# Turning the last token tiles and the shared expert blocks on TensorE, and taking weight conversions off the first batch's chain

## The chip, the cores and the metric

The kernel runs on one core of a Trainium2 chip. The metric is the device time of one execution in microseconds. PE below is the matrix engine (TensorE), PEld its weight load, DVE the vector engine, ACT the scalar engine, POOL the GpSimd engine, and SP the queue from which most transfers are issued, one after the other.

## What is computed

Three layers in a row: an attention with packed keys and values, a mixing layer with two Fourier transforms and a dense network, and a mixture of eight experts in which a token may take its predecessor's expert. All in float32.

```python
def attn(q, k, v, p):                      # 8 batches, 8 heads, 576 tokens, 64 wide; p: 32 packed rows
    packed = sm_attn(p, k, v)              # softmax attention
    return sm_attn(q, packed, packed)

def mix(x, w_ch1, w_ch2):                  # x: 8 x 576 x 512, w_ch1: 512 x 2048, w_ch2: 2048 x 512
    u = x + np.real(fft(fft(x, axis=1), axis=2))
    un = (u - mean(u)) / sqrt(var(u) + 1e-6)
    return u + maximum(un @ w_ch1, 0) @ w_ch2

def moe(x, w_gate, w_local, w1, w2):       # 8 experts, w1: 512 x 1024, w2: 1024 x 512
    for b, s in all tokens in order:
        fresh = argmax(x[b, s] @ w_gate)
        e = fresh if s == 0 or sigmoid(x[b, s] @ w_local) < 0.5 else prev_e
        prev_e = e
        out[b, s] = softmax(x[b, s] @ w_gate)[e] * (maximum(x[b, s] @ w1[e], 0) @ w2[e])
```

## The kernel before

Numbers are kept as pairs of float16 (high and low halves), so that a product takes three matmuls: high by high, high by low, low by high (PASS). The 4,608 tokens form 36 tiles of 128, called by their column 0 to 35; a batch has four whole tiles, and the rests of four batches together make two more (columns 16, 17 and 34, 35).

**First batch.** first_batch() is written in the order in which each engine runs it (the builder's scheduler is off there). It computes attention and mixing of batch 0. Its end is: P and Q products on PE (pq, L951), copies of Q to qs on ACT, combine(t) on DVE for tile pair t (L991: uu and ul are sums and differences of P and qs), stats(t) (mean and variance), level(t, j) (normalise to un, turn un with TensorE into the bank unt), high(t, j) and low(t, j) (the two float16 halves of the turned tokens, into `ut`). t is 0, 1 for 256 tokens each. While this runs, `weights(n)` draws n steps from the generator ch_weights (L281), which loads the mixing weights, chunk f of 16, unpacks them (k0, k1, k2 on DVE, L309 to L313), and lets split() (L277) make the halves of `w12`: high on ACT (L278), low on DVE (L279).

**Mixes.** Mix.mm1(f) makes a hidden chunk, 12 matmuls of 512 columns into hp (L1129); mm2(f) multiplies it back into acc (L1149). mm2 runs two chunks behind mm1. Between matmuls, tick() advances background generators by their rates: ch_weights at CW_RATE chunks' steps, attention of the next batch (attention(b + 1)), conversion of the expert weights into the DRAM tiles WS1 and WS2, after_mix of the mix before. From here on a scheduler places instructions, in the program's order unless an instruction has priority.

**Routing.** after_mix(tiles) (L1157) takes each finished tile: DVE finds its scale, ACT and DVE write its halves to a row tile `hl` (xh, three buffers, shared with the gathered rows xg), SP turns it with a DMA into `xt` (L1188, one buffer) and writes it to DRAM as XS (L1189). The logits of a tile are made from xt on PE (L1166, L1168), one tile behind. routing(gr) chooses experts and sorts tokens into blocks of 128, first for columns 0 to 17 and then, in finish_routing (after_mix of the last batch, columns 30 to 33, and routing(1)), beside the first expert blocks.

**Expert blocks.** The list `line` holds the 37 blocks in order: 34 with one expert and three shared by two experts of 64 tokens each (FIRST to FIRST + 2, which are 39 to 41). load_x gathers a block's rows and turns them by DMA (three blocks ahead); e1 (L1525) has 96 matmuls of 128 columns from `w1b` into ehp, e2 (L1586) 24 of 512 from `w2b` into eo. The loop over `line` issues e1 of block i + 1 before e2 of block i. Weight loads (L1517, four parts each) are issued by SP at places given by `first` and `second`. A shared block's e1_two (L1549) leaves its hidden rows hh unturned; turned(b) (L1570) turns them with 4 matmuls for each of four quarters (psum tile ht, copy to hx on ACT or DVE), and it runs inside e2 of the block before, between its matmuls.

Of the kernel before, what the change touches and what calls it, by code (L numbers as in the profile page):

```python
# [188 lines left out]
CW_RATE = 5  # L189
# [3 lines left out]
def _build(tc, nc, ctx, A, stop):  # L193
# [80 lines left out]
    held = []  # L274


    def split(dst_hi, dst_lo, src, scale):  # L277
        nc.scalar.activation(dst_hi, src, AF.Copy, scale=scale)  # L278
        nc.vector.scalar_tensor_tensor(dst_lo, src, scale, dst_hi, ALU.mult, ALU.subtract)  # L279

    def ch_weights():  # L281
# [15 lines left out]
        for f in range(16):  # L297
# [19 lines left out]
            split(w12[:, f, :, 0], w12[:, f, :, 1], t.rearrange("p (a n) -> p a n", a=2), 128.0)  # L317
# [408 lines left out]
    def first_batch():  # L726
# [201 lines left out]
        weights(5)  # L928
# [10 lines left out]
        weights(1)  # L939
# [36 lines left out]
        pq(1)  # L976
        x_mm(1, 1, psA)
# [13 lines left out]
        def combine(t):  # L991
# [3 lines left out]
            nc.vector.tensor_tensor(ul[R, :256], P[t][R, :256], qs[t][R, :256], op=ALU.subtract)  # L995
            if t == 0:
# [14 lines left out]
        def stats(t):  # L1011
# [10 lines left out]
            nc.gpsimd.tensor_tensor(out=rstd, in0=rstd, in1=mhalf, op=ALU.pow)  # L1022
            nbs[t] = wp.tile([128, 2], F32, tag="nb", name=f"nb0_{t}", bufs=2)
# [34 lines left out]
        weights(3)  # L1058
        combine(0)
        stats(0)  # L1060
        combine(1)
# [6 lines left out]
        stats(1)  # L1068
        level(1, 0)
        level(1, 1)  # L1070
        weights(1)
# [4 lines left out]
        combine(2)  # L1076
# [11 lines left out]
        split(wgh[:, :, 0], wgh[:, :, 1], wgf, 64.0)  # L1088
# [25 lines left out]
    class Mix:  # L1114
# [5 lines left out]
        def mm1(self, f):  # L1120
# [4 lines left out]
            hp = psM.tile([128, 512], F32, tag="h", name=f"hp{self.tiles[0][1]}_{f}")  # L1125
            n = 0
            for c in range(4):
                for (x, y) in PASS:
                    nc.tensor.matmul(hp[:, :ntok], w12[:, f, 0, x, 128 * c:128 * c + 128], ut[:, 4 * y + c, :ntok],  # L1129
                                     start=n == 0, stop=n == 11)  # L1130
                    n += 1
# [28 lines left out]
    def after_mix(tiles):  # L1160
# [12 lines left out]
        for j, (ut, col) in enumerate(tiles):  # L1173
# [311 lines left out]
    xg, xt, regs, hb = {}, {}, {}, {}  # L1485

# [38 lines left out]
    def e1(b, todo=()):  # L1525
# [3 lines left out]
        for fg in range(2):  # L1529
            hp = (psM, psO)[fg].tile([128, 512], F32, tag="ho"[fg], name=f"ehp{b}_{fg}")  # L1530
            for f in range(4):
                n = 0
                cols = slice(128 * f, 128 * f + 128)
                for c in range(4):
                    for (x, y) in PASS:
                        nc.tensor.matmul(hp[:, cols], w1b[r][:, 2 * c + fg, x, cols], xt[b][:, 4 * y + c],  # L1536
                                         start=n == 0, stop=n == 11, skip_group_check=True)
# [11 lines left out]
    def e1_two(b, todo=()):  # L1549
# [209 lines left out]
```

## Time and profile before

| | |
|---|---|
| median of 3 runs | 1425.25 us (1423.19 to 1433.6) |
| the profiled execution's own time | 1422.04 us |
| its span in the trace | 1420.0 us |
| mean granted PE clock, share of full speed | 0.987 |
| busy: PE, PEld, DVE, ACT, POOL | 1370.0, 791.2, 696.6, 516.1, 379.2 us |
| first batch's chain | 0 to about 62 us |
| end of the mixes, start of the expert blocks | about 983 us |

The first four numbers say how long it takes; the span leaves out about 2 us around the work. Busy times are sums of instructions' durations, so a busy engine may still run slowly: the granted clock says how fast PE was allowed to run in a stretch (1.0 is 2.4 GHz, 0.5 is 1.2 GHz). Views of the trace give for every instruction its start and duration and, in brackets, how long its engine had been idle before it and what released it.

### The profile page before, as it was taken

What the parts mean: (1) busy time and instruction counts of PE and PEld (TensorE: products, weight loads), DVE (VectorE), ACT (ScalarE), POOL (GpSimd) and SP (SyncE); (2) the same over time, 40 slices, a digit from 0 to 9 for tenths busy, and PEclk for the clock granted to TensorE, in tenths of its full rate; (3) what the DMA queues carried; (4) which work ended last, traced back from release to release, by engine and by line L of the source; (5) the groups of instructions that cost most, each with busy time, mean ns of one, the idle gap of its engine ahead of it and who ended that gap; (6) DMA issues with size and microseconds to landing.
All of it is one profiled execution on the core that took longest, in us unless ns stands there. A gap on an engine that the chain in (4) does not pass through costs nothing. (4 is left out here: it accounts for less than half of the span.)

```text
span 1420.0 us, 27686 instructions
## 1 busy us (share of the span) xinstructions
PE 1370.0 (96%) x10812; PEld 791.2 (56%) x10812; DVE 696.6 (49%) x1415; ACT 516.1 (36%) x950; POOL 379.2 (27%) x386
## 2 busy tenths in 40 slices
PE   7799999999999999999999999999999999999998
PEld 5553445444564544444544456446577777776654
DVE  5799856657534655665665755433561111111111
ACT  2443365554355545445445444211211111111111
POOL 1002243443422434343344252000121211212101
PEclk8999999999999999999999999999999999999999
DMA  7465384784567558558557457244969668858881
GB/s 262 160 211 197 91 237 124 172 237 121 137 171 209 156 150 214 142 147 219 139 153 197 121 148 166 58 194 129 261 145 318 180 190 250 264 149 239 280 275 44
DMA packets 223864, 257.67 MB, mean 181 GB/s; under 512 B 155887, under 2 KB 167279, under 8 KB 221040
## 3 DMA queue, kind: packets, MB, share of 16 engines
q1 hardware_dynamic: 217648, 236.44, 58.9%
q0 software_dynamic: 6080, 19.40, 4.2%
q8 instruction: 87, 1.43, 0.4%
q14 instruction: 49, 0.40, 0.1%
HBM read 267.52 MB, written 52.95 MB: 226 GB/s over the span
## 5 line engine op out<-in xcount | busy, mean ns | idle before, releaser
L1149 PE MATMUL acc<-w,ht 128*128 128x512 f16 x1728 | 409.5, 379 | 0.0
L1129 PE MATMUL hp<-ut,w 128*128 128x512 f16 x1536 | 365.9, 380 | 3.8 <-DMA ut<-unh 2.5
L1129 PEld LDWEIGHTS <-w 128*128 128x128 f16 x1920 | 183.1, 98 | 183.0 <-issue 11.4
L1149 PEld LDWEIGHTS <-ht 128*128 128x128 f16 x1728 | 165.7, 98 | 188.6 <-issue 8.6
L337 POOL TENSOR_TENSOR halfs<-stage,halfs 128x512 f16<-128x512 f32 x128 | 151.2, 1187 | 294.6 <-ACT halfs L336 279.0
L1597 PE MATMUL eo<-w2b,hx 128*128 128x512 f16 (+1 forms) x984 | 210.7, 382 | 0.0
L1536 PE MATMUL ehp<-xgt,w1b 128*128 128x128 f16 x3360 | 202.0, 220 | 3.2 <-DMA w1b<-WS 3.2
L1536 PEld LDWEIGHTS <-w1b 128*128 128x128 f16 x3360 | 194.0, 99 | 16.5 <-DMA w1b<-WS 3.7
L1545 DVE SCALAR_TENSOR_TENSOR hx<-ehp,hx 128x512 f16<-128x512 f32 x70 | 48.3, 691 | 294.5 <-ACT hx L1544 294.5
L1137 DVE SCALAR_TENSOR_TENSOR ht<-hp,ht 128x512 f16<-128x512 f32 (+1 forms) x160 | 101.2, 633 | 154.9 <-ACT ht L1136 153.9
L1136 ACT ACTIVATE ht<-hp 128x512 f16<-128x512 f32 (+1 forms) x160 | 88.1, 550 | 233.5 <-PE hp L1129 228.6
L1597 PEld LDWEIGHTS <-hx 128*128 128x128 f16 (+1 forms) x984 | 87.5, 100 | 99.9 <-issue 8.6
L1608 POOL DMA_INDIRECT out<-ys,sidx x38 | 41.0, 1079 | 291.3 <-ACT ys L1607 266.4
L1544 ACT ACTIVATE hx<-ehp 128x512 f16<-128x512 f32 x70 | 41.8, 597 | 163.7 <-PE ehp L1536 163.5
L1607 ACT ACTIVATE ys<-eo,scl 128x512 f32<-128x512 f32 x38 | 26.1, 687 | 170.5 <-PE eo L1597 170.5
L336 ACT CAST halfs<-stage 128x512 f16<-128x512 f32 x128 | 77.6, 615 | 9.3 <-DMA WS<-halfs 5.5
L1491 POOL DMA_INDIRECT xg<-XS,gidx x38 | 40.5, 1066 | 141.1 <-DVE sidx L1458 51.5
L335 ACT ACTIVATE stage<-stage 128x512 f32<-128x512 f32 x128 | 77.7, 623 | 0.2
L362 POOL TENSOR_TENSOR qh<-q,qh 128x1420 f16<-128x1420 f32 x12 | 34.6, 2882 | 51.6 <-ACT qh L361 51.5
L1129 PE MATMUL hp<-utr,w 128*128 128x256 f16 x384 | 47.1, 272 | 0.0
L574 PE MATMUL bp<-cst,eh 128*128 128x289 f16 (+1 forms) x168 | 26.2, 291 | 12.9 <-DVE lsum L1170 9.6
L539 POOL TENSOR_TENSOR eo<-ee 128x256 f32<-128x256 f32 (+1 forms) x21 | 17.0, 811 | 77.2 <-DVE ee L523 74.0
(408 smaller groups left out, 1388.2 us busy)
## 6 DMA issues: line engine op xcount, KB each, us to landing
w1b<-WS SPq DMA_DIRECT2D x156, 512.0 KB
w2b<-WS SPq DMA_DIRECT2D x156, 512.0 KB
stage<-in_w SPq DMA_DIRECT2D x64, 512.0 KB
WS<-halfs SPq DMA_DIRECT2D x128, 256.0 KB
q<-in_qd SPq DMA_DIRECT2D x16, 710.0 KB
v<-in_vd SPq DMA_DIRECT2D x16, 640.0 KB
k<-in_kd SPq DMA_DIRECT2D x16, 576.0 KB
XS<-xh SPq DMA_DIRECT2D x36, 256.0 KB
```

What stands on the lines that cost most here:

```text
L335: nc.scalar.activation(st[:, a], st[:, a], AF.Copy, scale=64.0 if k < 4 else 256.0)
L336: nc.scalar.copy(so[:, 0], st[:, a])
L337: nc.gpsimd.tensor_tensor(so[:, 1], st[:, a], so[:, 0], op=ALU.subtract)
L1129: nc.tensor.matmul(hp[:, :ntok], w12[:, f, 0, x, 128 * c:128 * c + 128], ut[:, 4 * y + c, :ntok], start=n == 0, stop=n == 11)
L1136: pace[1] = nc.scalar.activation(ht[:, 0, :ntok], hp[:, :ntok], AF.Relu).ins
L1137: pace[0] = nc.vector.scalar_tensor_tensor(ht[:, 1, :ntok], hp[:, :ntok], 0.0, ht[:, 0, :ntok], ALU.max, ALU.subtract).ins
L1149: nc.tensor.matmul(self.acc[j], ht[:, x, 128 * j:128 * j + 128], w12[:, f, 1, y], start=f == 0 and n == 0, stop=f == 15 and n == 2)
L1536: nc.tensor.matmul(hp[:, cols], w1b[r][:, 2 * c + fg, x, cols], xt[b][:, 4 * y + c], start=n == 0, stop=n == 11, skip_group_check=True)
L1544: nc.scalar.activation(ht[:, fg, 0], hp, AF.Relu)
L1545: nc.vector.scalar_tensor_tensor(ht[:, fg, 1], hp, 0.0, ht[:, fg, 0], ALU.max, ALU.subtract)
L1597: nc.tensor.matmul(op[rows], h[:, f // 4, x, c0 + rows.start:c0 + rows.stop], w2b[r + a][:, f, y], start=n == 0, stop=n == 23, skip_group_ ...
L1608: nc.gpsimd.indirect_dma_start(out=A["out"], out_offset=bass.IndirectOffsetOnAxis(ap=sidx[:, b:b + 1], axis=0), in_=ys, in_offset=None, bo ...
```

## The change

There are three edits. **A:** in first_batch, fewer weight steps stand ahead of the chain: six are drawn before the halves copies, none between Q and combine(0), and split() yields between its high and its low half, so the two can be placed apart. combine and stats become generators whose parts interleave; level(t, 0) runs on DVE for both t. begin(0) and begin(1) start mix chunks f = 0 and 1 on the first 256 tokens, before tile pair 1 is turned; mm1 then does the other 256 columns of these two. The rate CW_RATE goes from 5 to 6, since a chunk now has one step more. **B:** the last batch's four tiles (columns 30 to 33) are turned by four matmuls for each half and a copy on ACT and one on DVE, instead of a DMA; the last tile's logits follow after one step instead of four. **C:** the turns of a shared block go beside e1 of the next block, one quarter after each odd f, each placed behind the newest matmul of that e1, instead of beside e2 of the block before.

```diff
-CW_RATE = 5
+CW_RATE = 6
     def split(dst_hi, dst_lo, src, scale):
         nc.scalar.activation(dst_hi, src, AF.Copy, scale=scale)
+        yield
         nc.vector.scalar_tensor_tensor(dst_lo, src, scale, dst_hi, ALU.mult, ALU.subtract)
...
-        weights(5)
+        weights(6)
         halves(0, 0)
...
-        weights(1)
         qs, P, Q = {}, {}, {}
...
         pq(1)
+        weights(1)
         x_mm(1, 1, psA)
...
-            if (t, j) == (1, 0):
+            if j == 0:
                 nc.vector.tensor_scalar(un, ...
...
+        def begin(f):
+            hp = begun[f] = psM.tile([128, 512], F32, tag="h", name=f"hp0_{f}")
+            n = 0
+            for c in range(4):
+                for (x, y) in PASS:
+                    nc.tensor.matmul(hp[:, :256], w12[:, f, 0, x, 128 * c:128 * c + 128], ut[:, 4 * y + c, :256],
+                                     start=n == 0, stop=n == 11, skip_group_check=True)
+                    n += 1
-        weights(3)
-        combine(0)
-        stats(0)
-        combine(1)
+        whole(combine(0))
+        norm0, norm1, second = stats(0), stats(1), combine(1)
+        next(norm0)
+        next(second)
+        whole(norm0)
         level(0, 0)
...
         low(0, 1)
-        stats(1)
+        whole(second)
+        next(norm1)
+        weights(1)
+        whole(norm1)
+        begin(0)
         level(1, 0)
         level(1, 1)
-        weights(1)
+        weights(3)
+        begin(1)
         high(1, 0)
...
     # Mix.mm1
+            hp = begun.pop(f, None)
+            c0 = 0 if hp is None else 256
...
-                    nc.tensor.matmul(hp[:, :ntok], w12[...], ut[:, 4 * y + c, :ntok], ...
+                    nc.tensor.matmul(hp[:, c0:ntok], w12[...], ut[:, 4 * y + c, c0:ntok], ...
...
+    def turn_half(dst, src, nm, x):
+        tp = att(nm)
+        for c in range(4):
+            cols = slice(128 * c, 128 * c + 128)
+            nc.tensor.matmul(tp[:, cols], src[:, cols], idh, start=c == 0, stop=True, skip_group_check=True)
+        if x:
+            nc.vector.tensor_copy(dst, tp)
+        else:
+            nc.scalar.copy(dst, tp)
...
-            nc.sync.dma_start_transpose(out=xt, in_=hl)
+            if by_pe:
+                for x in range(2):
+                    turn_half(xt[:, 4 * x:4 * x + 4], hl[:, 512 * x:512 * x + 512], f"xtp{col}_{x}", x)
+            else:
+                nc.sync.dma_start_transpose(out=xt, in_=hl)
...
-        for _ in range(4):
+        for _ in range(1 if by_pe else 4):
             yield
         logits(tiles[-1][1])
...
     # e1, after the 12 matmuls of one f
+                if f % 2:
+                    next(beside, None)
...
     # turned
+                with tc.issue_after(newest[0]) if newest[0] is not None else nullcontext():
+                    turn_half(ht[:, fg, x], hh[:, fg, x], f"ht{b}_{fg}_{x}", x)
...
     # e2
-            if beside is not None and 2 <= f:
-                next(beside, None)
...
-    last = after_mix(prev.tiles)
+    last = after_mix(prev.tiles, True)
...
     # open_one(i), the e1 of line[i]
+        beside = turned(line[i - 1]) if i and line[i - 1] >= FIRST else iter(())
+        (e1_two if b >= FIRST else e1)(b, todo("e1", i), beside)
+        for _ in beside:
+            pass
```

What this does to the engines' orders is shown at three places. A row is a line of the program, the operation, and output<-inputs with the shape; numbers behind a name tell its batch, tile or chunk, and its allocation. Lines of the changed program stand one to some forty higher.

**The chain's head in the first batch.** First DVE before the change, around the first instruction of combine(0) (L994); raw1, halfs, stage and w12 belong to the weight conversion:

```order
L313 SCALAR_TENSOR_TENSOR raw1_177<-raw1_177,halfs_132 128x1024
L279 SCALAR_TENSOR_TENSOR w12_130<-raw1_177,w12_130 128x2x512
L309 TENSOR_SCALAR halfs_132<-stage_131 128x1024
L311 SCALAR_TENSOR_TENSOR halfs_132<-stage_131,halfs_132 128x1024
L994 TENSOR_TENSOR uu0_0_435<-P0_0_383,qs0_0_384 128x256
```

Then DVE of the change, where combine(0) is L996 to L1006 and X0_0 is added in stats(0):

```order
L315 SCALAR_TENSOR_TENSOR raw1_177<-raw1_177,halfs_132 128x1024
L996 TENSOR_TENSOR uu0_0_434<-P0_0_381,qs0_0_382 128x256
L997 TENSOR_TENSOR ul0_0_433<-P0_0_381,qs0_0_382 128x256
L1000 SCALAR_TENSOR_TENSOR ul0_0_433<-qs0_0_382,sgn_85,P0_0_381 128x256
L1006 SCALAR_TENSOR_TENSOR uu0_0_434<-qs0_0_382,sgn_85,P0_0_381 128x256
L1019 TENSOR_TENSOR uu0_0_434<-uu0_0_434,X0_0_1_366 128x512
```

And ACT in front of the same place, before the change (L932 copies halves, L969 to L973 make qs of tile pair 0):

```order
L932 ACTIVATE big0_256<-bp0_1_1_321 128x288
L278 ACTIVATE w12_130<-raw1_177 128x2x512
L969 COPY qs0_0_384<-zd0_382 1x257
L972 COPY qs0_0_384<-P0_0_383 128x255
L973 COPY qs0_0_384<-zd0_382 1x257
```

and with it, down to the copy for tile pair 1 (L964):

```order
L934 ACTIVATE big0_256<-bp0_1_1_321 128x288
L970 COPY qs0_0_382<-zd0_380 1x257
L973 COPY qs0_0_382<-P0_0_381 128x255
L974 COPY qs0_0_382<-zd0_380 1x257
L902 ACTIVATE big0_256<-att0_2_399 128x4x32
L964 COPY qs0_1_385<-P0_1_384 128x255
L279 ACTIVATE w12_130<-raw1_177 128x2x512
```

The low half of chunk 1 and the unpacking of chunk 2 (three DVE instructions) no longer stand between DVE's L313 and combine(0), and the high half of chunk 1 has moved behind the qs copies of both tile pairs on ACT.

**SP while the last tiles are routed.** SP before, from the last part of w1b for the third block on; xt31 to xt33 are the last batch's turned tiles, xh their row tiles, xgt a block's turned rows:

```order
L1517 DMA w1b2_10097<-WS1_128 128x2048
L1188 DMA_TRANSPOSE xt31_10257<-xh31_10217 128x8x128
L1189 DMA XS_127<-xh31_10217 128x1024
L1495 DMA_TRANSPOSE xgt3_10282<-xg3_10278 128x8x128
L1517 ISA
L1517 DMA w1b0_9398<-WS1_128 128x2048
```

and with the change:

```order
L1560 DMA w1b2_10121<-WS1_128 128x2048
L1231 DMA XS_127<-xh31_10252 128x1024
L1538 DMA_TRANSPOSE xgt3_10328<-xg3_10324 128x8x128
L1560 ISA
L1560 DMA w1b0_9422<-WS1_128 128x2048
```

The transpose of the tile is gone from the queue; the write of its rows keeps its place among the loads.

**PE at a shared block.** PE before, in e2 of block 29 (eo29): turns of the hidden rows of shared block 39 (ht39 from hh39), ahead of the next matmuls of eo29:

```order
L1597 MATMUL eo29_15426<-w2b0_9400,hx29_15202 128x512
L1577 LDWEIGHTS hh39_15345
L1577 MATMUL ht39_0_0_15437<-c16_97,hh39_15345 128x128
...
L1577 MATMUL ht39_0_1_15446<-c16_97,hh39_15345 128x128
L1597 LDWEIGHTS hx29_15202
L1597 MATMUL eo29_15426<-w2b0_9400,hx29_15202 128x512
...
L1577 MATMUL ht39_1_0_15455<-c16_97,hh39_15345 128x128
```

and with the change, in e1 of block 30 (ehp30):

```order
L1579 MATMUL ehp30_0_15531<-xgt30_15268,w1b0_9422 128x128
L1192 LDWEIGHTS hh39_15413
L1192 MATMUL ht39_0_0_15595<-c16_97,hh39_15413 128x128
...
L1579 LDWEIGHTS w1b0_9422
L1579 MATMUL ehp30_0_15531<-xgt30_15268,w1b0_9422 128x128
...
L1192 MATMUL ht39_0_1_15627<-c16_97,hh39_15413 128x128
L1579 LDWEIGHTS w1b0_9422
L1579 MATMUL ehp30_1_15635<-xgt30_15268,w1b0_9422 128x128
```

The turns have moved behind all of eo29, into the following block's matmuls.

## Rows read from the trace of the kernel before

**Rows 1.** Page, part 1: busy us, share of the span, instructions
```profile
PE 1370.0 (96%) x10812; PEld 791.2 (56%) x10812; DVE 696.6 (49%) x1415; ACT 516.1 (36%) x950; POOL 379.2 (27%) x386
```

**Rows 2.** Waits of PE; columns: us in total, times, longest us
```profile
PE ehp L1536 <- DMA w1b<-WS: 3.2, 3, 1.5
PE lp L1166 <- DMA xt<-xh: 2.8, 3, 1.8
...
PE hp L1129 <- DVE w L279: 1.2, 2, 0.9
PE ht L1577 <- ACT hx L1582: 1.2, 2, 0.6
...
PE ht L1577 <- DVE hh L1566: 0.8, 2, 0.4
```

**Rows 3.** Busy by stretch: us, PE PEld DVE ACT POOL, PEclk, DMA, GB/s
```profile
50.00:60.00 10.00, 6.55 (x31) 5.29 (x32) 7.29 (x20) 5.52 (x11) 1.55 (x3) 0.66 0.00 1
70.00:80.00 10.00, 9.14 (x44) 3.96 (x42) 9.42 (x13) 5.20 (x10) 0.00 (x0) 1.00 0.76 187
995.00:1000.00 5.00, 4.33 (x23) 1.86 (x24) 1.85 (x4) 1.32 (x2) 0.00 (x0) 0.69 1.16 283
1030.00:1035.00 5.00, 3.29 (x31) 3.12 (x32) 4.83 (x13) 0.00 (x0) 1.29 (x2) 0.60 0.82 155
```

**Rows 4.** Timeline, 39 to 47: start us, duration, instruction, idle before and releaser
```profile
40.68 1.02 PE L955 MATMUL P<-g,big 128*128 128x255 f32 x4
41.97 1.12 ACT L278 ACTIVATE w<-raw 128x1024 f16<-128x1024 f32 x1 [2.93 <-DVE raw L313]
43.13 1.22 DVE L279 SCALAR_TENSOR_TENSOR w<-raw,w 128x1024 f16<-128x1024 f32 x1 [1.19 <-ACT w L278]
43.97 0.36 ACT L973 COPY qs<-zd 1x257 f32<-1x257 f32 x1
...
46.13 0.42 DVE L994 TENSOR_TENSOR uu<-P,qs 128x256 f32<-128x256 f32 x1
```

**Rows 5.** Timeline, 53 to 61
```profile
53.01 3.78 PE L1037 MATMUL unt<-ident,un 128*128 128x128 f32 x16 [5.43 <-ACT un L1034]
...
58.09 0.59 ACT L1049 CAST ut<-unt 128x512 f16<-128x512 f32 x1 [0.18 <-PE unt L1048]
...
59.45 1.16 PE L1037 MATMUL unt<-ident,un 128*128 128x128 f32 x8 [0.19 <-ACT un L1034]
```

**Rows 6.** Timeline of PE at 178, batch 1's first matmuls
```profile
178.26 1.67 PE L1129 MATMUL hp<-ut,w 128*128 128x512 f16 x7 [2.47 <-DMA ut<-unh]
```

**Rows 7.** Page, part 5: busy us, mean ns of one, idle before
```profile
L1129 PE MATMUL hp<-utr,w 128*128 128x256 f16 x384 | 47.1, 272 | 0.0
```

**Rows 8.** Timeline of PE, 983 to 1038
```profile
983.20 10.66 PE L1536 MATMUL ehp<-xgt,w1b 128*128 128x128 f16 x188
995.67 0.18 PE L1166 MATMUL lp<-wgh,xt 128*128 128x18 f16 x1 [1.81 <-DMA xt<-xh]
...
996.11 6.17 PE L1597 MATMUL eo<-w2b,hx 128*128 128x512 f16 x20
...
1022.70 5.34 PE L1597 MATMUL eo<-w2b,hx 128*128 128x512 f16 x24
...
1032.05 5.62 PE L1536 MATMUL ehp<-xgt,w1b 128*128 128x128 f16 x51 [1.53 <-DMA w1b<-WS]
```

**Rows 9.** Timeline of SP's issues, 986 to 1018
```profile
986.88 3.84 SPq L1188 DMA_TRANSPOSE xt<-xh  x1
...
1007.51 1.62 SPq L1188 DMA_TRANSPOSE xt<-xh  x1
...
1010.04 2.23 SPq L1517 DMA_DIRECT2D w2b<-WS  x4
...
1014.38 3.08 SPq L1517 DMA_DIRECT2D w1b<-WS  x4
```

**Rows 10.** Timeline of ACT at 1001
```profile
1001.76 0.72 ACT L1180 ACTIVATE xh<-uu,rsc 128x512 f16<-128x512 f32 x1 [3.40 <-DMA XS<-xh]
```

More of the change, by code (lines that the diff above doesn't have):

```diff
@@ L1057, in first_batch, with whole @@
             U[0, t] = tuple(wp.tile([128, 512], F32, tag="U", name=f"u{'lu'[j]}0_{t}", bufs=8) for j in range(2))
-        weights(3)
-        combine(0)
-        stats(0)
-        combine(1)
+        def whole(gen):
+            for _ in gen:
+                pass
[12 more added lines that the diff above has]
+        whole(norm0)
         level(0, 0)
@@ L1075, in first_batch @@
         low(1, 1)
-        combine(2)
+        whole(combine(2))
         for lu, r in ((1, slice(64, 96)), (0, slice(32, 64))):
@@ L1087, in first_batch @@
         nc.sync.dma_start(c32, A["c32"])
-        split(wgh[:, :, 0], wgh[:, :, 1], wgf, 64.0)
+        for _ in split(wgh[:, :, 0], wgh[:, :, 1], wgf, 64.0):
+            pass
     bg = []
@@ L1124, in mm1 @@
                 next(cw)
-            hp = psM.tile([128, 512], F32, tag="h", name=f"hp{self.tiles[0][1]}_{f}")
+            hp = begun.pop(f, None)
+            c0 = 0 if hp is None else 256
+            if hp is None:
+                hp = psM.tile([128, 512], F32, tag="h", name=f"hp{self.tiles[0][1]}_{f}")
             n = 0
@@ L1128, in mm1 @@
                 for (x, y) in PASS:
-                    nc.tensor.matmul(hp[:, :ntok], w12[:, f, 0, x, 128 * c:128 * c + 128], ut[:, 4 * y + c, :ntok],
-                                     start=n == 0, stop=n == 11)
+                    nc.tensor.matmul(hp[:, c0:ntok], w12[:, f, 0, x, 128 * c:128 * c + 128], ut[:, 4 * y + c, c0:ntok],
+                                     start=n == 0, stop=n == 11, skip_group_check=True)
                     n += 1
@@ L1158, in mm2, with after_mix @@
             tick(0.25)
-    def after_mix(tiles):
+    def turn_half(dst, src, nm, x):
[7 more added lines that the diff above has]
+            nc.scalar.copy(dst, tp)
+    def after_mix(tiles, by_pe=False):
         xt = None
@@ L1523, in load_w2, with e1 @@
         weights(b, w2b, WS2, k0, k1)
-    def e1(b, todo=()):
+    def e1(b, todo=(), beside=iter(())):
         ht = M["q"].tile([128, 2, 2, 512], F16, tag="hx", name=f"hx{b}", bufs=3)
@@ L1535, in e1 @@
                     for (x, y) in PASS:
-                        nc.tensor.matmul(hp[:, cols], w1b[r][:, 2 * c + fg, x, cols], xt[b][:, 4 * y + c],
-                                         start=n == 0, stop=n == 11, skip_group_check=True)
+                        newest[0] = nc.tensor.matmul(hp[:, cols], w1b[r][:, 2 * c + fg, x, cols], xt[b][:, 4 * y + c],
+                                                     start=n == 0, stop=n == 11, skip_group_check=True).ins
                         n += 1
@@ L1547, in e1, with e1_two @@
         hb[b] = ht
-    def e1_two(b, todo=()):
+    def e1_two(b, todo=(), beside=None):
         hh = M["q"].tile([128, 2, 2, 512], F16, tag="hx", name=f"hh{b}", bufs=3)
@@ L1573, in turned, with e2 @@
             for x in range(2):
-                tp = att(f"ht{b}_{fg}_{x}")
-                for f in range(4):
-                    cols = slice(128 * f, 128 * f + 128)
-                    nc.tensor.matmul(tp[:, cols], hh[:, fg, x, cols], idh, start=f == 0, stop=True,
-                                     skip_group_check=True)
-                if x:
-                    nc.vector.tensor_copy(ht[:, fg, x], tp)
-                else:
-                    nc.scalar.copy(ht[:, fg, x], tp)
+                with tc.issue_after(newest[0]) if newest[0] is not None else nullcontext():
+                    turn_half(ht[:, fg, x], hh[:, fg, x], f"ht{b}_{fg}_{x}", x)
                 yield
         hb[b] = ht
-    def e2(b, todo=(), beside=None):
+    def e2(b, todo=()):
         h = hb.pop(b)
```

15 lines of the change are left out of this document (9 added, 6 removed).

## The prediction

> **What bounds the kernel now.** I read the page first: PE is busy 96% of the span [rows 1], so a microsecond is worth having only where PE itself stands or runs slowly. Then PE's waits, longest first, and where each falls. Five of those lines lie where this change works [rows 2]: 3.2 us for expert weights (w1b), 2.8 us for the last batch's rows turned by DMA (xt), 1.2 us for converted mix weights, and 1.2 and 0.8 us for the turned halves of shared blocks. Then busy time by stretch, for the granted clock: 0.66 in 50:60, 0.69 in 995:1000, 0.60 in 1030:1035, so in each of these PE ran for a while at 1.2 GHz instead of 2.4, each time after it had stood [rows 3]. The same rows show DVE busy 9.42 of 10 us in 70:80: the first mix is nearly DVE's stage too. Three places follow: the first batch's start (A), the last tiles' routing with the first expert blocks (B), the shared blocks (C).
>
> **A, the first batch.** DVE begins combine(0) at 46.13 [rows 4]. What it needs is ready sooner: the last of tile 0's Q matmuls ends at 40.68 + 1.02 = 41.70, and after that two copies of 0.36 us on ACT remain. Both now queue behind the conversion that ACT does at 41.97 for 1.12 us, and DVE puts conversions from 43.13 to 46.13 ahead of combine. Both leave the chain (the order rows show it), so combine can start at about 42.5, 3.6 us earlier. Then PE's turns of tile 0: 16 matmuls take 3.78 us at 53.01, while the later 8 take 1.16 at full clock [rows 5]; if PE has stood 1.6 us instead of 5.43 I expect full clock, 16 in 2.3 us, 1.5 us less. With the two un tiles made on DVE and ACT side by side (an estimate of 0.4 us), the first 256 tokens, complete at 58.09 + 0.59 = 58.68 now, are there some 5.5 us earlier. The two half groups then fill PE's wait for tile 1.
>
> What survives of 5.5? From below: the 3.0 us of DVE conversions come back inside a stage where DVE is 94% busy, which leaves 2.5; and batch 1's attention, much of which runs on DVE, may keep all but 1 of it. Nothing below zero: DVE's work is the same, only its waits are fewer. From above: 5.5, the 1.2 us of waits for weights and 1.3 us of PE's other stands in that stretch, together 8. I take 5.2, about midway between 2.5 and 8: the new PE order puts acc and pps matmuls between the matmuls that need only the high half of a weight and those that need the low half, so PE need not stand for DVE; but at 178.26 PE waits 2.47 us for batch 1's turned tokens [rows 6], and there the lead of DVE's chain counts, not PE's. What is late next is that wait, which grows as PE comes earlier. Against it: 24 matmuls of 512 columns become 48 of 256. At 47.1/384 = 0.123 us each [rows 7] against 5.34/24 = 0.2225 for 512 columns [rows 8], that is 24 x 0.023 = 0.6 us. **A gives 4.6 us, between 1 and 8.**
>
> **B, the last tiles.** Taken away: the stand of 1.81 us at 995.67. The half clock behind it: 20 matmuls in 6.17 us, where 24 take 5.34 at full clock, so 1.7 us. The three stands for w1b, 3.2 us [rows 2]. The half clock behind those: 51 matmuls in 5.62 us, at 10.66/188 = 0.0567 us each worth 2.9, so 2.7 us [rows 8]. Together 9.4 us.
>
> Why should the w1b stands go, which the change doesn't name? SP issues in order. The loads waited for are the four at 1014.38; ahead of them, since 986.88, stand four xt transposes (3.84 us to issue the first, 1.62 the last) and four loads of w2b at 1010.04 [rows 9]. The transposes go, and the row tiles behind them (xh) are finished sooner, since the freed ticks pull the routing forward by about one block. I expect w1b's issue some 8 to 10 us earlier, while PE comes to that block at most 3 us earlier. It landed 1032.05 - 1014.38 = 17.7 us after its issue; 8 us earlier covers 3.2 of stands.
>
> Added: 32 matmuls of 128 columns at 0.0567, 1.8 us. ACT and DVE get four copies each, beside a PE that doesn't wait for them. And stands at the turns, which PE now meets in order: none at best; at worst the present 1.81 at each of two places. I take 1.0 in all, nearer to none, because the first two tiles' rows don't wait for a buffer. **B gives 9.4 - 1.8 - 1.0 = 6.6 us.** Lowest 0.7, if the w1b stands and their half clock stay; highest 7.6.
>
> A rule speaks against the turns' price. The Trainium skill, "TensorE: Matmul & The Clock Gate", section "Back-to-back issue gap", gives about 81 ns for each matmul of 128 columns in a stream of loads and matmuls. The rows show 57 ns here for just such a stream [rows 8], and the measurement decides; by the page the turns would cost 2.6 us and the whole sum would be 0.8 smaller.
>
> **C, the shared blocks.** Two of the three stood 0.6 + 0.4 us each for their turned halves, 2.0 us [rows 2]. The same 16 turns of each now stand one by one among the next block's 96 matmuls, 15 to 24 of them (0.9 to 1.4 us) from one turn to the next, which covers a copy of 0.6 to 0.7. **C gives 2.0 us,** between 1 and 2.
>
> **Sum.** 4.6 + 6.6 + 2.0 = 13.2 us. Against the profiled execution's own 1422.04 that is 1408.8; the median of the runs shown, 1425.25, lies 3.2 above it, so I forecast 1425.25 - 13.2 = 1412.
>
> **Rivals.**
> *The weights stay late.* If w1b is late because the transfers are slow (DMA share 0.82 to 1.16 in these stretches [rows 3]) and not because SP issues late, its 5.9 us stay: a gain of 7.3, 1418. For it: 17.7 us from issue to use. Against: eight issues of weights and four transposes lie ahead, and half of that goes.
> *DVE takes the start back.* The deferred conversions hold batch 1's chain, and at 178 only 1 us is left: a gain of 9.6, 1416. For: 94% busy. Against: PE's new order.
> *The turns wait for buffers (slower).* Row tiles share three buffers, and the fourth tile is made at 1001.76, after ACT stood 3.40 us for a row's write-back to land [rows 10]. PE now reaches that tile's turn at about 983.2 + 192 x 0.0567 + 13 x 0.2225 + the turns and stands, some 999 to 1000. If write-backs land as now it stands 3 us, and half clock behind it costs 1.7 more: the gain shrinks to 8.5, 1417. It decides the sign from 13 us of stands and half clock on: if both of the last tiles stood for the 8.8 us that the first xt takes now (986.88 to 995.67) and ran at half clock behind it (1.7 each), that is 21 us less the 1.0 counted, a kernel 7 us slower, 1432. Against: the write-backs are issued earlier too, no longer behind a transpose. The Trainium skill, "Advanced Engine Details and Errata", section "X-Bar Transpose (TRN2)", says that transposing DMAs are as fast as plain ones; by that the 8.8 us would be backlog, which write-backs meet as well, and it speaks for this rival. Only SP's 3.84 us of issue for the first transpose [rows 9] speaks against the rule here; no row tells its transfer from the backlog.
>
> **How the numbers follow.** Forecast case 0.68; weights late 0.14; start taken back 0.12; buffers, slower, 0.04; anything else 0.02. A difference of 1% (14.3 us) is about what a measurement of this kernel can tell from none. The forecast lies 1.1 us short of it: a little more in A suffices, so half of the forecast case, 0.34, and 0.02 besides are faster by over 1%: 0.36. Slower by over 1%: 0.04. Within 1%: 0.60. Low end: A 8, B 7.6, C 2 give 1407.6, and the fastest run lies 2 under the median: 1405. High end: weights late and A at 1, a gain of 3.7: 1421. The forecast case alone: 1406 to 1417.
>
> **What would show it.** A: combine at 42 to 43 and a granted clock of 1.0 in 50:60; hp matmuls of 256 columns before 56; a longer wait for ut at about 175. B: no wait for xt or w1b; w1b's issues before 1008; a clock of 1.0 in 990:1035; stands at xtp under 1 us. C: no wait at ht. It is wrong if PE waits for w (the low halves) by over 3 us in 60:100, if w1b is still waited for, or if xtp of the last two tiles stands over 3 us.

## The result, and the profile after

| kernel | runs | median us | before beside it, us | ratio, 95% interval |
|---|---|---|---|---|
| the change | 6 | 1414.13 (1407.62 to 1416.94) | 1425.74 | 0.9904 (0.9877 to 0.9931) |
| the change, second time | 6 | 1410.10 | 1423.37 | 0.9903 (0.9878 to 0.9928) |
| the change, third time | 6 | 1418.20 | 1426.94 | 0.9932 (0.9908 to 0.9957) |

The change is 0.7 to 1.0% faster, 9 to 14 us; the forecast was 13.2 us and 1412. So the time fell where it was expected, just under the line of 1%. It did not come from where it was expected: the edits alone, below, gave about 5.8 (A), 0.7 (B) and 5.1 us (C) where 4.6, 6.6 and 2.0 stood in the sum.

The profiled execution of the change took 1416.94 us (span 1414.9, mean granted clock 0.991); it is the slowest of its six, only 5.1 us under the profiled execution of before. Page, part 1, as in [rows 1]:

```profile
PE 1368.8 (97%) x10868; PEld 790.2 (56%) x10868; DVE 702.1 (50%) x1420; ACT 518.4 (37%) x953; POOL 376.0 (27%) x386
```

PE has 56 matmuls more (32 turns, 24 halves of mix chunks) and is still busy 1.2 us less; it ran some 25 us of the span at 1.2 GHz where it had been some 37. Its waits, to be held against [rows 2] (us in total, times, longest):

```profile
PE unt L1041 <- DVE un L1036: 2.4, 2, 1.5
PE s L385 <- DVE ru L676: 1.9, 1, 1.9
PE tabf L1465 <- DVE stage L1476: 1.7, 1, 1.7
...
PE hp L1156 <- DMA ut<-unh: 1.6, 1, 1.6
PE ep L1310 <- DVE e L1300: 1.6, 2, 1.2
...
PE ff L1286 <- DVE fk L1269: 0.6, 1, 0.6
...
PE xtp L1192 <- ACT xh L1218: 0.5, 2, 0.3
```

The waits for w1b and ht are gone from this list, and that for xt in the routing of the last tiles. New are one of 1.9 us for DVE in front of batch 1 (s, attention of batch 2), and those of the last tiles' routing: ep grew from 1.0 to 1.6, and tabf, which did not wait at all before, now stands 1.7 us for a table that DVE builds. Busy time by stretch, the columns and stretches of [rows 3] and 170:180 besides:

```profile
50.00:60.00 10.00, 6.95 (x56) 5.55 (x58) 8.93 (x19) 5.23 (x9) 2.36 (x3) 1.00 0.30 100
70.00:80.00 10.00, 9.79 (x70) 4.38 (x69) 9.84 (x14) 4.28 (x9) 0.00 (x0) 1.00 0.97 282
170.00:180.00 10.00, 6.54 (x31) 1.82 (x28) 6.50 (x14) 0.72 (x1) 2.14 (x3) 0.72 0.28 53
995.00:1000.00 5.00, 4.71 (x50) 2.68 (x48) 2.60 (x6) 2.24 (x4) 0.00 (x0) 1.00 1.08 261
1030.00:1035.00 5.00, 4.88 (x39) 3.00 (x38) 5.00 (x9) 0.69 (x1) 0.16 (x1) 1.00 0.87 193
```

The granted clock is 1.00 in all three stretches that ran at 0.60 to 0.69 before. But 170:180 is at 0.72: behind the stands in front of batch 1, PE now runs at 1.2 GHz for a while. The first batch's chain, which answers to [rows 4] and [rows 5] (timeline: start us, duration, instruction, idle before):

```profile
41.17 1.03 PE L956 MATMUL P<-g,big 128*128 128x257 f32 x4
...
44.82 0.42 DVE L996 TENSOR_TENSOR uu<-P,qs 128x256 f32<-128x256 f32 x1 [0.65 <-PE X L910]
...
51.32 2.05 PE L1041 MATMUL unt<-ident,un 128*128 128x128 f32 x16 [1.51 <-DVE un L1036]
...
54.53 0.27 PE L1071 MATMUL hp<-ut,w 128*128 128x256 f16 x1
...
175.49 3.57 PE L1156 MATMUL hp<-ut,w 128*128 128x512 f16 x8 [1.58 <-DMA ut<-unh]
```

combine starts 44.82 - 41.17 = 3.65 us after the first P matmul; before it was 46.13 - 38.95 = 7.18. The 16 turns take 2.05 us instead of 3.78. Batch 1 (the last row, which answers to [rows 6]) starts at 175.49 instead of 178.26, although this execution reached P 2.2 us later: in 16:36 PE ran at 1.2 GHz for 17.1 us, in the profile of before for 13.6 (worked out from the granted clock in stretches of 2 us, as all such times below). Since that first stretch differs from execution to execution, I measure sections from now on:

| profile | first P matmul to batch 1's first hp | from there to the first expert matmul | from there to the sixth expert block's eo | last 13 of the eo groups |
|---|---|---|---|---|
| before | 139.3 | 804.9 | 81.4 | 103.9 |
| the change | 134.3 | 807.8 | 78.9 | 98.7 |
| second time | 134.5 | 809.5 | 79.2 | 98.7 |
| third time | 134.5 | 807.9 | 79.5 | 98.5 |

Each is the distance between the starts of two matmuls in the trace (us); the last column runs from the 29th group of 24 eo matmuls to the last matmul's end.

Between the third and the fourth section lies a stretch that none of them counts, from the sixth eo to the 29th group. It takes 245.7 us before, in each edit alone and in the second profile of the change, but 248.3 in its first and 249.9 in its third, and 246.6 to 251.5 in the other kernels below that combine edits. Seven of the ten profiles with more than one edit stand there for 0.7 to 1.9 us at about 1,300 us. In the third profile the row names the expert weights, in the others it names no transfer (1.26, then 0.79 in the first profile):

```profile
1300.71 0.51 PE L1579 MATMUL ehp<-xgt,w1b 128*128 128x128 f16 x6 [1.26 <-DMA w1b<-WS]
```
```profile
1301.87 0.51 PE L1579 MATMUL ehp<-xgt,w1b 128*128 128x128 f16 x6 [0.79 <-PE ehp L1579]
```

So w1b is no longer waited for where the tiles are routed, but in one profile at least it is later on, and a part of the gain is lost there. No run tests why.

### The profile page after: what moved, and what is told of

It is laid out like the page before. It is cut to its first block, busy times and chain, and to the rows that moved or that the text cites. A ratio compares the mean times of both kernels' runs of the same rounds, so it can differ in the third digit from the quotient of the medians.

```text
span 1414.9 us, 27811 instructions
## 1 busy us (share of the span) xinstructions
PE 1368.8 (97%) x10868; PEld 790.2 (56%) x10868; DVE 702.1 (50%) x1420; ACT 518.4 (37%) x953; POOL 376.0 (27%) x386
## 5 line engine op out<-in xcount | busy, mean ns | idle before, releaser
L1156 PE MATMUL hp<-ut,w 128*128 128x512 f16 (+1 forms) x1536 | 366.1, 379 | 2.2 <-DMA ut<-unh 1.6
L1156 PEld LDWEIGHTS <-w 128*128 128x128 f16 x1920 | 182.6, 98 | 180.5 <-issue 10.9
L1635 PE MATMUL eo<-w2b,hx 128*128 128x512 f16 (+1 forms) x984 | 207.5, 379 | 0.1
L338 ACT CAST halfs<-stage 128x512 f16<-128x512 f32 x128 | 77.6, 615 | 9.2 <-DMA WS<-halfs 5.4
```

Of the source, the lines that this page charges most:

```text
L338: nc.scalar.copy(so[:, 0], st[:, a])
L1156: nc.tensor.matmul(hp[:, c0:ntok], w12[:, f, 0, x, 128 * c:128 * c + 128], ut[:, 4 * y + c, c0:ntok], start=n == 0, stop=n == 11, skip_gro ...
L1635: nc.tensor.matmul(op[rows], h[:, f // 4, x, c0 + rows.start:c0 + rows.stop], w2b[r + a][:, f, y], start=n == 0, stop=n == 23, skip_group_ ...
```

## The experiments

### The three edits, each alone

Kernel before with the hunks of one edit: A (first batch), B (last tiles), C (shared blocks).

> The kernel before with edit A alone. The prediction: 4.6 us faster (1 to 8). The theory from the two traces: batch 1's first matmuls start about 2.8 us earlier (175.5 against 178.3), because its tokens come at the end of a chain on DVE, and that is all that is left of a lead of 7 to 14 us in batch 0's matmuls; so 2 to 3 us faster where no half clock follows the stands in front of batch 1, and none where one does (0.1 in the profile of the change). Rival: A's gain is kept in full, then batch 1's acc matmuls start 4 us or more earlier and the time falls by 4 us or more.

> The kernel before with edit B alone. The prediction: 6.6 us faster (0.7 to 7.6). The theory from the traces: 2 to 3 us faster from the start of the expert blocks to their fifth eo (it was 2.5 us there in the profile of the change), because the routing of the last columns now meets PE with some 4 us of stands for DVE (ff, ep, tabf) that the stands for weights used to cover. Rival: the routing's stands come from A's shift and not from B; then B alone shows no stand of over 1 us at ep or tabf and gains 5 us or more.

> The kernel before with edit C alone. The prediction: 2.0 us faster (1 to 2). The theory from the traces: 4 to 5 us faster in the last 120 us, of which 2.6 are the stands at ht with their fill, and the rest are matmuls of unlike shape that no longer alternate (0.09 us at each switch between pairs of 64 columns of weights and whole ones). Rival: only the stands count, then 2.0 to 2.6 us and as many switches as before.

> The change once more, beside its parts. If the parts add, its gain is the sum of the gains of the three, by the prediction 13.2 us, by the traces of one execution each about 2.5 (A) + 2.5 (B) + 4.5 (C) = 9.5 us. A second profile also shows which half clock stretches come back: if the one at 174 to 181 us is missing here, it is a matter of the execution and not of the change.

| kernel | runs | median us | ratio to before (29 runs, 1423.37) | in us |
|---|---|---|---|---|
| A alone | 12 | 1416.83 | 0.9959 (0.9942 to 0.9976) | 5.8 faster (3.4 to 8.3) |
| B alone | 12 | 1422.93 | 0.9995 (0.9975 to 1.0015) | 0.7 faster (-2.1 to 3.6) |
| C alone | 12 | 1417.25 | 0.9964 (0.9945 to 0.9983) | 5.1 faster (2.4 to 7.8) |
| all | 6 | 1410.10 | 0.9903 (0.9878 to 0.9928) | 13.8 faster (10.2 to 17.4) |

The parts add to 11.6 us, which lies within the interval of the whole; the 9.5 read from the traces lies just below it. The sections of their profiles:

| profile | P to batch 1 | to the experts | to the sixth eo | last 13 eo groups |
|---|---|---|---|---|
| A alone | 135.5 | 808.8 | 81.3 | 103.9 |
| B alone | 139.9 | 804.6 | 78.8 | 104.0 |
| C alone | 140.7 | 804.9 | 77.6 | 98.5 |

**A.** Batch 1 starts 135.5 us after the first P with A and 139.3 to 140.7 without it. The rows (first matmul of batch 1, for A, B and C alone in turn):

```profile
169.89 3.57 PE L1156 MATMUL hp<-ut,w 128*128 128x512 f16 x8 [1.59 <-DMA ut<-unh]
```
```profile
174.21 1.67 PE L1129 MATMUL hp<-ut,w 128*128 128x512 f16 x7 [2.52 <-DMA ut<-unh]
```
```profile
175.32 3.15 PE L1129 MATMUL hp<-ut,w 128*128 128x512 f16 x7 [2.48 <-DMA ut<-unh]
```

None of the three ran at half clock near 16:36, so the starts can be compared as they stand. Eight matmuls take 3.57 us with A and seven 1.67 in the second row: that is the 1.2 GHz behind the stands. The third row shows that it can come without A too.

So the start comes 3.8 to 5.2 us earlier, not 2.8, and the time falls by 5.8 us, not by 2 to 3: the theory ahead of this run was too low, and its rival fits better. Taken apart between the same two points, in the profiles of the change, of A alone and of the later kernels with an equal start: PE's stands come to 9.4 to 10.9 us with A and 13.9 to 15.0 without, what the half clock costs to 0 to 0.6 and 3.4 to 5.2 us, and all the rest, in which PE now does more, to 124.0 to 124.8 and 120.6 to 121.4.

**B.** PE's stands in the routing section, of B alone and then of C alone, which still turns by DMA:

```profile
981.68 0.40 PE L1165 MATMUL xtp<-c,xh 128*128 128x128 f16 x4 [0.30 <-ACT xh L1191]
991.84 0.40 PE L1165 MATMUL xtp<-c,xh 128*128 128x128 f16 x4 [1.15 <-ACT xh L1191]
1001.40 0.22 PE L1259 MATMUL ff<-c,fk 128*4 128x128 f16 x1 [0.37 <-DVE fk L1244]
1005.06 0.17 PE L1283 MATMUL ep<-c,e 4*128 4x4 f16 x1 [0.60 <-DVE e L1273]
1019.03 0.60 PE L1438 MATMUL tabf<-stage,owf 128*128 128x238 bf16 x4 [1.66 <-DVE stage L1449]
```
```profile
992.82 0.18 PE L1177 MATMUL lp<-wgh,xt 128*128 128x18 f16 x1 [1.96 <-DMA xt<-xh]
998.15 0.18 PE L1177 MATMUL lp<-wgh,xt 128*128 128x18 f16 x1 [0.42 <-DMA xt<-xh]
1011.55 0.22 PE L1259 MATMUL ff<-c,fk 128*4 128x128 f16 x1 [0.50 <-DVE fk L1244]
1015.22 0.17 PE L1283 MATMUL ep<-c,e 4*128 4x4 f16 x1 [0.60 <-DVE e L1273]
1029.48 0.60 PE L1438 MATMUL tabf<-stage,owf 128*128 128x238 bf16 x4 [1.49 <-DVE stage L1449]
```

The tabf stand of B alone, 1.66 us, refutes the rival that it came from A's shift. The section without B is the shorter one, 77.6 against 78.8 us: it stands 5.0 us where B stands 4.1, and has no turns. And it has no wait for w1b, which the prediction credited to B. In its place stands tabf, 1.49 us. In A alone, which also turns by DMA, it is the other way round:

```profile
1027.37 0.34 PE L1563 MATMUL ehp<-xgt,w1b 128*128 128x128 f16 x3 [1.38 <-DMA w1b<-WS]
1028.47 4.65 PE L1563 MATMUL ehp<-xgt,w1b 128*128 128x128 f16 x51 [0.76 <-DMA w1b<-WS]
```

There w1b is waited for, tabf is not, and the clock falls twice (0.83 in 990:1000, 0.89 in 1030:1040). In this section every one of the 14 profiles has one of the two stands and none has both: PE waits either for the weights or for DVE's table. The profiles that turn by DMA (before, A alone, C alone and "without B" below) run the same instructions there in the same order on every engine, so it is their timing, and not an order that an edit brought, that decides between the two. No such kernel was profiled twice.

**C.** The last stretch is 98.5 to 98.7 us with C as written and 103.9 or 104.0 without it, in every profile. Of the 5.5 us, 2.0 are the stands at ht, and 0.6 more is what a matmul takes behind such a stand. Most of the rest is order. Counted in the trace, PE changes between matmuls on the whole array and pairs on 64 columns of it 50 times before and 32 times with C, and what these starts take beyond a plain one falls from 4.9 to 3.1 us. Changes between whole matmuls of 128 and of 512 columns grow from 20 to 29, but they cost nothing that the starts show. And of the matmuls that belong in a pair, 0.21 us for one as for two, ten ran alone before and four with C, 0.6 us less. That makes 5.0; 0.5 us stays unaccounted.

### Batch 1's start: more work on DVE, less work on DVE, no early matmuls

```diff
 # more
-                            nc.vector.tensor_scalar(m, top, 3, 0x3FFFFFF8, ...)
+                            for _ in range(1 + (f >= 3)):
+                                nc.vector.tensor_scalar(m, top, 3, 0x3FFFFFF8, ...)
 # less
-            yield from split(w12[:, f, :, 0], w12[:, f, :, 1], t..., 128.0)
+            if f < 3:
+                yield from split(w12[:, f, :, 0], w12[:, f, :, 1], t, 128.0)
+            else:
+                nc.scalar.activation(t, t, AF.Copy, scale=128.0)
+                nc.scalar.copy(w12[:, f, :, 0], t)
+                yield
+                nc.gpsimd.tensor_tensor(out=w12[:, f, :, 1], in0=t, in1=w12[:, f, :, 0], op=ALU.subtract)
 # no early matmuls
-        begin(0)
-        begin(1)
```

> The change, with the first unpacking step of chunks 3 to 15 done twice on DVE (0.69 us each, about 12 of them before batch 1's tokens are turned, 8 us; the same values). If DVE's chain is what keeps batch 1 from starting, its first matmuls come 6 to 8 us later than in the change, PE's stands in front of them grow by that, and the time by 6 us or more. If PE is the bound there and the 5.8 us of A alone are kept by PE's own lead, DVE has room: the start moves by 2 us at most.

> The change, with the low halves of chunks 3 to 15 taken off DVE (1.22 us each, some 15 us in all): ACT scales the chunk in place and copies the high half, POOL, busy 0 to 5 of 10 us there, subtracts (an estimate of 2.4 us each from 1.18 us for half that size). If DVE's chain holds batch 1's start back, the 3.5 us of stands ahead of it (173 and 175 us in the change) and with them the half clock behind go, and the kernel is 4 to 7 us faster than the change. If PE is the bound, nothing moves by over 1 us. If POOL's chain is too slow for the mix, hp waits for w from POOL and it is slower.

> The change without begin(0) and begin(1), so mix chunks 0 and 1 run whole once all 512 tokens are turned; DVE's and ACT's orders stay as in the change. By the prediction most of A is DVE's lead: batch 1's first matmuls start within 1 us of the change's, and the time is the same within 1 us, but for a half clock at 46 to 56 us, which the longer stands in front of the turns could bring back (2 to 3 us). Rival: the early matmuls carry A's gain; then 3 us or more are lost and batch 1 starts later by as much.

The kernel before took 1426.81 us beside them (27 runs).

| kernel | median us | ratio | P to batch 1 | to the experts |
|---|---|---|---|---|
| more work on DVE | 1423.21 | 0.9967 (0.9943 to 0.9992) | 144.2 | 808.6 |
| less work on DVE | 1428.50 | 1.0009 (0.9988 to 1.0029) | 146.6 | 809.2 |
| no early matmuls | 1421.97 | 0.9966 (0.9951 to 0.9980) | 142.6 | 804.8 |

Some 8 us more on DVE move batch 1's start by 9.7 us: DVE's chain does hold it. The sum of DVE's durations between the two points says the same. It is 147.9 us here, and 138.1 to 138.3 in the three profiles of the change, more than the 134.3 to 134.5 us of the stretch itself (neighbouring instructions overlap a little); before, it was 137.5 of 139.3. So A took waiting out of DVE, not work. One part of the expectation failed: the stands right in front of batch 1 grew only from 3.5 to 4.3 us, and the rest came earlier, as small stands (16.9 us in all, 9.6 to 10.0 in the change) and as 7.9 us at 1.2 GHz. The change itself did not run beside these three; against its ratios elsewhere the loss is 0.35 to 0.64%, 5 to 9 us, about the 6 expected.

Taking the low halves off DVE did not help, and this run says nothing on what DVE's load costs, since it makes a longer wait elsewhere. Waits of PE in that kernel:

```profile
PE hp L1163 <- POOL w L326: 11.2, 8, 2.2
...
PE hp L1163 <- ACT w L324: 2.5, 3, 1.1
```

POOL needs 2.1 to 3.1 us for what DVE did in 1.22, and ACT comes twice; the mix of batch 0 waits 13.7 us for weights. The stand in front of batch 1 did shrink, from 3.5 to 1.3 us, but PE came later by itself.

Without the early matmuls the expectation failed: batch 1's start is 8 us later than in the change, not within 1 us, and 4.9 to 9 us are lost. The rows of that kernel (timeline):

```profile
53.82 3.58 PE L1041 MATMUL unt<-ident,un 128*128 128x128 f32 x16 [3.00 <-DVE un L1036]
...
180.12 0.59 PE L1154 MATMUL hp<-ut,w 128*128 128x512 f16 x1 [3.19 <-DMA ut<-unh]
```

and the row of the change that answers to the first:

```profile
57.33 2.05 PE L1041 MATMUL unt<-ident,un 128*128 128x128 f32 x16 [0.87 <-DVE un L1036]
```

PE stands 3.00 us in front of the second turns where it stood 0.87 with begin, and then turns at half clock (3.58 us, 2.05 with begin). DVE's durations sum to 139.1 us, 0.9 more than in the change, in a stretch that is 8 us longer, so it is DVE's waiting that grew. My reading is that PE is late with every hp from there on, and that DVE, which runs its list in order, has batch 1's instructions behind the halves of those hp; no run shows this link by itself. The clock has a share: PE runs 10.4 us of this stretch at 1.2 GHz, in the change 1.2 at most. By this reading PE's early work and DVE's chain are one lead, not two.

### What holds C, what B is worth, two rates

```diff
 # turns not held (the change's turned)
-                with tc.issue_after(newest[0]) if newest[0] is not None else nullcontext():
+                with nullcontext():
 # without B: the change, with after_mix and its call as before
-    last = after_mix(prev.tiles, True)
+    last = after_mix(prev.tiles)
 # slower routing
-R1_RATE = 1.2
+R1_RATE = 1.0
 # slower conversion
-CW_RATE = 6
+CW_RATE = 5
```

> The change without the hold on the shared blocks' turns (they are written beside the next block's e1 but no longer placed behind its newest matmul), so the scheduler puts them among the block's own matmuls again, as before. If what C gains comes from turns that stand one by one behind e1's matmuls, without stands and with few switches between matmuls of unlike shape, all of it goes: stands at ht of 0.4 to 0.6 us are back, and the time is 4 to 5 us over the change. If moving them into e1 alone were enough, it stays within 1 us of the change.

> The change without edit B: the last tiles are turned by DMA again. If B is worth nothing (0.7 us alone, and 4 us of stands for the routing's DVE work where there were 6 for xt and w1b, less 1.8 us of turns), it stays within 2 us of the change. By the prediction it loses 6.6 us. Rival: B pays only once A and C are there (half clock stretches behind the xt stands, near 992 and 1030 us, come back without it): then 3 to 4 us are lost, and the profile shows them.

> The change with the rate of the routing beside the expert blocks at 1.0 steps per tick instead of 1.2, so more matmuls of PE lie between two of its steps. If its stands (ff, ep, tabf, xtp, 4.1 to 4.6 us in all) come from steps that follow too closely for DVE's part in them, they shrink by 2 us or more and the time by 1 to 2 us, a version better than the change. If one step's DVE work is by itself longer than what PE has between two steps at any rate near this, the stands stay within 1 us and the time within 1 us.

> The change with the weight conversion's rate at 5 steps per tick instead of 6 (one step more per chunk now). DVE's conversions then spread over more of batch 0, and batch 1's attention gets DVE earlier. If it is DVE's order that holds batch 1 back, its start comes 1 to 3 us earlier or the conversions turn up as waits of hp for w; if the rate only shifts work that must all be done before, the start moves by under 1 us and the time by under 1 us.

> The change once more, on the chip of the other three. Faster than before by 0.97% (0.9904 and 0.9903 so far), some 13.7 us; the stands in front of batch 1 are 1.9 and 1.6 us and those of the routing beside the expert blocks 4.1 to 4.6 us again, since stands have come back to 0.1 us in every profile so far, and only the half clock stretches differ.

| kernel | median us | before beside it | ratio | P to batch 1 | to the experts | to the sixth eo | last 13 eo groups |
|---|---|---|---|---|---|---|---|
| turns not held | 1417.06 | 1426.81 | 0.9921 (0.9899 to 0.9944) | 134.3 | 806.7 | 79.2 | 103.9 |
| without B | 1414.79 | 1426.94 | 0.9922 (0.9895 to 0.9949) | 134.3 | 808.8 | 77.6 | 98.5 |
| slower routing | 1414.03 | 1426.94 | 0.9910 (0.9883 to 0.9936) | 134.5 | 807.0 | 80.9 | 98.5 |
| slower conversion | 1418.89 | 1426.94 | 0.9938 (0.9914 to 0.9961) | 138.1 | 804.6 | 80.0 | 98.5 |

**Turns not held.** The last stretch is back at 103.9 us, and so are the stands; of the kernel with C alone the same place stands below it (second shared block, timeline):

```profile
1349.74 0.38 PE L1192 MATMUL ht<-c,hh 128*128 128x128 f16 x4 [0.61 <-ACT hx L1196]
1350.51 0.40 PE L1192 MATMUL ht<-c,hh 128*128 128x128 f16 x4 [0.39 <-DVE hh L1611]
...
1352.80 2.36 PE L1635 MATMUL eo<-w2b,hx 128*64 128x512 f16 x11
1355.09 0.51 PE L1579 MATMUL ehp<-xgt,w1b 128*128 128x128 f16 x6
1355.53 3.01 PE L1635 MATMUL eo<-w2b,hx 128*64 128x512 f16 x18
```
```profile
1354.15 0.39 PE L1165 MATMUL ht<-c,hh 128*128 128x128 f16 x4
1354.38 1.00 PE L1552 MATMUL ehp<-xgt,w1b 128*128 128x128 f16 x15
1355.21 0.39 PE L1165 MATMUL ht<-c,hh 128*128 128x128 f16 x4
1355.43 1.50 PE L1552 MATMUL ehp<-xgt,w1b 128*128 128x128 f16 x24
1356.78 0.39 PE L1165 MATMUL ht<-c,hh 128*128 128x128 f16 x4
1357.09 5.37 PE L1608 MATMUL eo<-w2b,hx 128*64 128x512 f16 x48
```

Held, the shared block's 48 matmuls run in one piece in 5.37 us, 0.11 each, since two of a pair run side by side; not held, they come in pieces between others, with 50 changes between pairs and whole matmuls as before. So it is the hold, not the place in the program, that carries C. The median does not show it by itself: 0.9921 lies between the change's 0.9903 and 0.9932. The section, which profiles with the same order repeat within 0.3 us, says 5.2.

**Without B** nothing is lost against the change beside it: 3.4 us less in the median (interval -5.4 to 2.0), 77.6 us in the routing section, the stands xt 2.63 and tabf 1.80, no w1b, no half clock. It issues the w1b loads as late after the first expert matmul as the kernel before did (31.2 us) and yet does not wait for them there. The prediction's 6.6 is excluded.

**The routing's rate** does not set its stands: 4.8 us at 1.0 steps per tick as against 4.0, 4.5 and 4.7 at 1.2 in the three profiles of the change (ep alone 2.0, tabf 1.6). The kernel was 4.2 us faster than the change beside it in the median, but the interval (-6.5 to 0.8) holds zero and no section explains it (the routing's own is longer, 80.9 us, with 3.4 us at 1.2 GHz), so I don't call it better.

**The conversion's rate** moved batch 1's start by 3.6 us, later, which neither branch had; the waits of hp for w that the first branch named did turn up, 1.1 us on ACT's half where the change has 0.2. And yet the time is the same (0.7 us slower, -2.1 to 4.2). From batch 1 on it needed 804.6 us and the change 807.8 to 809.5.

**The change, third time,** gained 0.68% where 0.97 was expected, just outside its interval (0.43 to 0.92). The stands in front of batch 1 came back to 0.1 us, 1.9 and 1.6; those of the routing did not, 4.7 us with 0.81 at one xtp (0.17 and 1.42 in the two profiles ahead of it).

## Why the prediction was right, and where its steps were not

**The sum** was right by errors that nearly cancel: B 6 us too high, C 3 us too low, A 1 us too low. That it met the number was luck.

**A** was sized right in the median: 4.6 foretold, 5.8 measured (3.4 to 8.3). The lead of 3.6 us at combine is there (3.5), the turns ran at full clock (2.05 us, 2.3 foretold), and batch 1 starts 4 to 6 us earlier (134.3 to 135.5 against 139.3 to 140.7), where 5.2, the middle between two bounds, had been taken as what survives. Two of its sentences fell. "There the lead of DVE's chain counts, not PE's": without the early matmuls the whole lead is gone, so both carry it. And the lead at batch 1 is not the gain: the profiles that start batch 1 after 134.3 to 135.5 us need 806.7 to 809.5 us from there to the experts, those without A 804.6 to 804.9, so 1.8 to 5.0 are given back, in part through half clock at 168 to 182 (3.4 to 6.8 us in five of them; "turns not held" and "slower routing" have none there). Outside stands and half clock this section takes 789.5 to 790.1 us in all of them; the half clock costs 0 to 1.7 us without A and 1.7 to 4.5 with it, the stands take 13.6 to 14.6 and 14.7 to 16.1. The prediction named the longer wait at 178 but not that a stand there can bring the clock down. From the first P to the experts A then leaves some 2 us in the mean of the profiles (944.3 to 945.6 without, 941.0 to 944.3 with), less than the 5.8 of the medians, though the interval reaches down to 3.4. What fits the difference is the clock of the runs that were only timed: each run lists its mean granted clock, 0.988 in the mean over 29 runs of before and 0.9925 over 12 of A alone. Within the 29 runs the time goes with it, from 1427 us at 0.984 to 1417 at 0.992, about 10.7 us for each 0.01, so 0.0044 is worth some 4.7 us. One stretch that A removes is known (46 to 60, present in before, B alone and C alone, 6.8 us at 1.2 GHz, absent with A as long as the early matmuls are there). Which others the timed runs had is not recorded, and this stays open.

**B** failed: 0.7 us (-2.1 to 3.6) for 6.6. The step that failed is "taken away: ... together 9.4". It took 3.2 us of w1b stands and 4.4 us of half clock as a fixed cost of the kernel before. They come and go: of the four profiles that turn by DMA, before and A alone need 81.4 and 81.3 us for the section, with a wait for w1b and half clock twice, and C alone and "without B" need 77.6 with neither. The nine that turn by TensorE and have no half clock there need 78.8 to 80.4, 79.4 in the mean. So B costs some 1.9 us where the clock stays up anyway, about what its turns take (1.8), and saves as much where it would have fallen. The second failed step is "and stands at the turns ... I take 1.0 in all": the turns did stand little (0.5 to 2.0 us), but the routing behind them stands too, ff, ep and tabf 2.6 to 4.0 us, of which only 0.9 were there before. Where PE does not wait for w1b it waits for DVE's tables, so the w1b stand seems to have been their cover. The step on SP's queue was right in direction only: w1b was issued at 1009.33, 5 us earlier and not 8 to 10, and "without B" shows that no stand need follow without it.

The 81 ns that the Trainium skill, "TensorE: Matmul & The Clock Gate", section "Back-to-back issue gap", gives for a matmul of 128 columns in such a stream would have made B's turns dearer. The runs agree with the row instead: 15 such matmuls take 1.00 us and 24 take 1.50, 56 ns each from the difference of these two rows of C alone.

**C** had the right mechanism and the wrong size: 2.0 us foretold, 5.5 in the section, 5.1 in the time. The term counted PE's stands only. It left out what a stand costs behind it (0.6), the 18 changes between whole matmuls and pairs that go (1.8) and three pairs that ran apart (0.6); what each of these costs could be read in the trace of before.

**The rivals.** "The weights stay late" and "the turns wait for buffers" did not happen: no stand for w1b in this stretch, and at most 1.4 us at one xtp in the change's profiles (1.7 in one experiment), though ACT did wait 0.60 and 1.26 us for a row's write-back. "DVE takes the start back" is wrong at 178, where 4 to 6 us are left; what is given back behind it is mostly the clock's. **What would show it**: the clock, the 256-column matmuls before 56 (54.53) and no wait at ht came as written. combine came at 44.82 and not at 42 to 43, since this execution reached P 2.2 us later. The wait for ut did not grow, it is 1.6 us where it was 2.5, but a new one of 1.9 us stands in front of it. The issue of w1b came too late, and xtp stood under 1 us in the first profile (0.5) but not in the second and third (1.7 and 1.1).

## What to carry to other kernels

A stand and its half clock that one profile shows is a cost only if a second profile shows it again; take two profiles of the kernel before, and price what differs between them at its frequency. When a wait is removed, look which engine was catching up behind it: here DVE's tables took the place of the weights, and the gain was nil. And look at the order of matmuls as well as at the gaps between them: a hold of one small group behind another's newest matmul gave as much as the whole first edit.

## What the runs showed of the hardware that was not expected

The same kernel varies by 10 us (29 runs of before, 1417.3 to 1427.3) while the first batch's stands repeat to 0.1 us (the four in front of the turns and the early matmuls: 1.51, 0.46, 0.29, 0.87 us in the change and 1.52, 0.46, 0.29, 0.87 the second time). Later ones do not: ep stood 1.20, 0.60 and 1.45 us in the three profiles of the change. What the time goes with is the granted clock: in 16:36 PE ran at 1.2 GHz for 17.1, 13.6, 10.2, 3.4 or 0 us in different profiles, whichever edits were in. The stands in front of batch 1 (1.9 and 1.6 us) were followed by 1.2 GHz in five profiles and not in three others with the same stands.

A change between matmuls on the whole array and pairs on 64 columns of it costs PE 0.09 to 0.12 us beyond a plain start. The last whole matmul of 128 columns ahead of a pair takes 0.149 us to the next start, where 0.056 is usual, and one of 512 columns 0.309, where 0.216 is usual; ahead of a whole matmul of the other width both keep their usual time (starts of single matmuls in the last 104 us of the trace of before). Two matmuls on 64 columns each start 4 ns apart and take 0.21 us together; one alone takes as long.
